# Decode attention plus MLP on one core: in each step a slice's scores are issued ahead of its values, and the values one slice later

## The chip, the cores and the metric

The kernel runs on one core of a Trainium2 chip. The core has a matrix engine (PE, TensorE), a vector engine (DVE, VectorE), an activation engine (ACT, ScalarE), GpSimd (POOL), and SyncE (SP), which here issues nearly all DMA transfers. Each engine works off its own list of instructions in order, and waits on semaphores where another engine or a transfer must be done first. PEld in a profile is PE's loading of weights (the stationary operand). The metric is the device time of one execution in microseconds (us).

## The reference, cut to what matters

One decode step (one token, batch 4) of two parallel blocks on the same normalised input:

```python
x = A_x                                   # (4, 1, 576) bf16
xn = layernorm(x)
# A: attention over the last W = 2048 positions of the cache, 32 query heads on 16 key/value heads of 128
q = (xn @ wq) as (4, 32, 1, 128)
scores = q . k_cache[:, :, -2048:, :] * 128 ** -0.5
o = softmax(scores) . v_cache[:, :, -2048:, :]
A = o as (4, 1, 4096) @ wo                # wo: 4096 x 576
# B: with one token the shifted groups of the mixer are zero, so hs = 0 and x1 = xn
B = xn + gelu(layernorm(xn) @ w3) @ w4    # w3: 576 x 4608, w4: 4608 x 576
out = x + A + B
```

What must be read is some 87 MB: 16 heads of keys and of values, 2 MB each, wq and wo of 4.7 MB each, w3 and w4 of 5.3 MB each. w1 and w2 aren't read.

## The kernel before

**Loads.** `load_kv` (L103) loads the keys of one key/value head for all four batches as one 128 x 8192 bf16 tile (2048 KB), the values likewise. Keys and values share a pool of six such buffers. The order is K0 K1 K2 V0 K3 V1 K4 V2 and so on to K15 V13 V14 V15; a quarter of wo goes ahead of every fourth V, w3 after V2, and w4 at the very end in six pieces (L141; the first has 18 of 36 blocks of rows, the last two have one each). All stand in SP's list, in that order. A load waits until the buffer that it takes over is free: K(t+3) takes that of K(t), free when DVE has turned its last slice; V(h+3) takes that of V(h), free when PE has used its last slice. `flush_loads` issues them at the end of each step.

**Steps.** One loop over t = 0 to 15 runs four heads at different stages, with hm = t-1, hv = t-2, hf = t-3, hp = t-4, and each step has four slices s = 0 to 3:

- `k_transpose` (L225): DVE turns a quarter of K(t), one slice ahead of its use, into one of three buffers kt;
- `k_mask` (L329) and `k_scores` (L338): PE adds the scores of slice s of head t into the PSUM tile S, four matmuls of 512 columns a slice. Two S tiles exist;
- softmax of head hm, spread over the slices: `sm_max` (L344, L346, DVE) at s = 0, `sm_maxT` (L351, PE) and `sm_neg` (L356, DVE) at s = 1, `sm_sub` (L360, PE) and `sm_exp` (L366, ACT) at s = 2, `sm_turn` (L372, DVE: the probabilities PT) and `sm_den` (L376, PE) at s = 3, `sm_rec` (L381, DVE) in the next step;
- `pv` (L390): PE multiplies slice s of PT(hv) with slice s of V(hv) into O, four matmuls that lie side by side in the array. The first one of a step waits for V(hv);
- head hf: `o_scale` (L397, ACT), `o_turn` (L403, PE), `o_sum` (L413, DVE); every fourth head `o_spread` (L422, PE), `o_pick` (L432, L435, DVE) and, a step later, `o_proj` (L183, PE: the product with a quarter of wo, into acc).

In step 7 the first product of the MLP (`mlp_g`, L456) with its turn and activation is put between. The schedule is manual: every engine's list has the instructions in the order in which the loop issues them.

**After the loop** the heads that are left are finished: the softmax of head 15, the values of heads 14 and 15, `o_turn`, `o_sum` and `o_spread` (L422, the tile R). Then `mlp_out` (L183) multiplies by w4 piece by piece, with `o_proj` of the last heads behind the first piece. These are pairs of 288-column matmuls with 8 rows of output, one of each pair into acc and one into acc_odd, which lie side by side in the array. ACT copies acc_odd (L606), DVE adds it to acc (L613), and SP stores 4.5 KB.

Of the kernel before, what the change touches and what calls it, by code (L numbers as in the profile page):

```python
# [22 lines left out]
def kernel(  # L23
# [32 lines left out]
    NSL = 4  # L56
# [165 lines left out]
    def k_transpose(h, s):  # L222
        src = kv_tiles["K", h][:].bitcast(I32)[:, s * SC:(s + 1) * SC, :].rearrange("p c (ib i) -> p ib c i", i=QD)
        kt = ktp.tile([P, 2, SC, QD], I32, tag="kt")
        nc.vector.transpose(out=kt[:], in_=src)  # L225
        kts[h, s] = kt
# [100 lines left out]
    def k_mask(h):  # L327
        S_ps[h] = ps_s.tile([P, NW], F32, tag="S", name="S")
        nc.tensor.matmul(out=S_ps[h][:].rearrange("p (c k) -> p c k", k=QD), lhsT=ohT[:],  # L329
                         rhs=negbig[:].unsqueeze(1).to_broadcast([B, SC, QD]),  # L330
                         start=True, stop=False, skip_group_check=True)

    def k_scores(h, s):
        kt = kts.pop((h, s))[:].bitcast(BF16)
        for ie in range(4):
            ib, e = divmod(ie, 2)
            z0 = (h * 4 + ie) * P + ZP - s * NJ
            nc.tensor.matmul(out=S_ps[h][:], lhsT=qz[:, z0:z0 + P],  # L338
                             rhs=kt[:, ib, :, e:2 * QD:2].rearrange("p c k -> p (c k)"),
                             start=False, stop=False, skip_group_check=True)  # L340

    def sm_max(h):
        mx = small.tile([P, 1], F32, tag="mx")
        nc.vector.reduce_max(out=mx[:], in_=S_ps[h][:], axis=AX.X)  # L344
        dm = small.tile([P, NG], BF16, tag="dm")
        nc.vector.tensor_scalar(out=dm[:], in0=sel_g[:], scalar1=mx[:, 0:1], scalar2=None, op0=ALU.mult)  # L346
        st["dm", h] = dm

    def sm_maxT(h):
        mg = ps_m.tile([NJ, NG], F32, tag="m", name="mg")  # L350
        nc.tensor.matmul(out=mg[:], lhsT=sel_jb[:], rhs=st.pop(("dm", h))[:], start=True, stop=True)  # L351
        st["mg", h] = mg

    def sm_neg(h):
        nm = small.tile([NJ, 1], BF16, tag="nm")
        nc.vector.reduce_max(out=nm[:], in_=st.pop(("mg", h))[:], axis=AX.X, negate=True)  # L356
        st["nm", h] = nm

    def sm_sub(h):
        nc.tensor.matmul(out=S_ps[h][:], lhsT=j_row[:], rhs=st.pop(("nm", h))[:, 0:1].to_broadcast([NJ, NW]),  # L360
                         start=False, stop=False, skip_group_check=True)

    def sm_exp(h):
        E[h] = ptp.tile([P, SC, QD], BF16, tag="e", name="E")
        rs = small.tile([P, 1], F32, tag="rs", bufs=3)
        nc.scalar.activation(out=E[h][:].rearrange("p c k -> p (c k)"), in_=S_ps.pop(h)[:], func=ACT.Exp, scale=scale,  # L366
                             accum_out=rs[:])
        st["rs", h] = rs

    def sm_turn(h):  # L370
        PT[h] = ptp.tile([P, SC, QD], BF16, tag="pt", name="PT")
        nc.vector.transpose(out=PT[h][:], in_=E.pop(h)[:])  # L372

    def sm_den(h):
        dn = ps_m.tile([P, 1], F32, tag="m", name="dn")
        nc.tensor.matmul(out=dn[:], lhsT=same_j[:], rhs=st.pop(("rs", h))[:], start=True, stop=True)  # L376
        st["dn", h] = dn

    def sm_rec(h):
        rd = small.tile([P, 1], F32, tag="rd", bufs=4)  # L380
        nc.vector.reciprocal(out=rd[:], in_=st.pop(("dn", h))[:])  # L381
        st["rd", h] = rd

    def pv(h, s):
        if s == 0:
            O_ps[h] = ps_o.tile([P, NSL, Dh], F32, tag="O", name="O")
        vn = kv_tiles["V", h][:].rearrange("p (s c) d -> p s c d", s=NSL)
        for g in range(NQD):
            c = s * NQD + g
            nc.tensor.matmul(out=O_ps[h][g * QD:(g + 1) * QD], lhsT=PT[h][:, c, :], rhs=vn[:, :, c, :],  # L390
                             start=(s == 0), stop=False, skip_group_check=True)
        if s == NSL - 1:
            PT.pop(h)

    def o_scale(h):
        O_sb[h] = bigp.tile([P, NSL, Dh], F32, tag="big", name="O_sb")
        nc.scalar.activation(out=O_sb[h][:], in_=O_ps.pop(h)[:], func=ACT.Copy, scale=st.pop(("rd", h))[:, 0:1])  # L397

    def o_turn(h):
        oT = ps_m.tile([P, NSL, P], F32, tag="m", name="oT")  # L400
        o = O_sb.pop(h)
        for s in range(NSL):
            nc.tensor.transpose(out=oT[:, s, :], in_=o[:, s, :], identity=ident_w[:, s * NJ:s * NJ + P])  # L403
        st["oT", h] = oT

    def o_sum(h):
        oT = st.pop(("oT", h))
        v = oT[:].rearrange("p s (g x) -> p (s g) x", g=NQD)[:, :, 0:NJ].rearrange("p g (b r) -> p b r g", r=rep)
        k = h % WOQ
        if k == 0:  # L410
            st["on"] = small.tile([P, WOH, B], BF16, tag="on", name="on")
        with nc.allow_low_precision("summed in float32"):
            nc.vector.reduce_sum(out=st["on"][:, k * rep:(k + 1) * rep, :].rearrange("p r b -> p b r"),  # L413
                                 in_=v, axis=AX.X)

    def o_spread(h):
        if h % WOQ < WOQ - 1:
            return
        on = st.pop("on")
        R = ps_m.tile([P, WOR, WOH, B], F32, tag="m", name="R")  # L420
        for i in range(WOR):
            nc.tensor.matmul(out=R[:, i].rearrange("p h b -> p (h b)"),  # L422
                             lhsT=sel_wo[:, i].rearrange("p h d -> p (h d)"),
                             rhs=on[:].rearrange("p h b -> p (h b)"), start=True, stop=True)
        st["R"] = R

    def o_pick(h):
        if h % WOQ < WOQ - 1:
            return
        R = st.pop("R")  # L430
        mk = small.tile([P, WOR, WOH, B], BF16, tag="mk")
        nc.vector.tensor_tensor(out=mk[:], in0=R[:],  # L432
                                in1=own[:].unsqueeze(1).unsqueeze(3).to_broadcast([P, WOR, WOH, B]), op=ALU.mult)
        with nc.allow_low_precision("one term is not zero"):
            nc.vector.reduce_sum(out=op[:, :, ROWS], in_=mk[:].rearrange("p i h b -> p i b h"), axis=AX.X)  # L435

    def o_proj(h):
        if h % WOQ < WOQ - 1:
            return
        for i in range(0, WOR, 2):  # L440
            acc_matmuls([(op[:, i + u, :], wo_tiles[h // WOQ][:, i + u, :]) for u in range(2)])
# [74 lines left out]
    for t in range(Hkv):  # L516
        hm, hv, hf, hp = t - 1, t - 2, t - 3, t - 4
        for s in range(NSL):
            if s == NSL - 1 and hm >= 0:
                sm_turn(hm)  # L520
            n = t * NSL + s + 1
            if n < Hkv * NSL:
                k_transpose(*divmod(n, NSL))

            if s == 0:
                if hm >= 0:
                    sm_max(hm)
                if hv >= 0:
                    sm_rec(hv)
                if hp >= 0:  # L530
                    o_pick(hp)
                if hf >= 0:
                    o_scale(hf)
                k_mask(t)
            elif s == 1 and hm >= 0:
                sm_maxT(hm)
            elif s == 2:
                if hm >= 0:
                    sm_sub(hm)
                    sm_exp(hm)  # L540
                if hf >= 0:
                    o_sum(hf)
            elif s == 3 and hm >= 0:
                sm_den(hm)
            if hv >= 0:
                pv(hv, s)
            k_scores(t, s)
            if s == 1:
                if hm >= 0:
                    sm_neg(hm)  # L550
                if hf >= 0:
                    o_turn(hf)
                if hp >= 0:
                    o_proj(hp)
            elif s == 3 and hf >= 0:
                o_spread(hf)
            if t == G_AT:
                if s < 3:
                    mlp_g(s)
                if s > 0:  # L560
                    mlp_turn(s - 1)
                if s == NSL - 1:
                    mlp_act()
        pos["free"] += 1
        if hv >= 0:
            pos["free"] += 1
        flush_loads()
# [77 lines left out]
```

## Time and profile before

| | us |
|---|---|
| median of six runs | 211.99 |
| the six runs | 211.51, 211.71, 211.73, 212.25, 212.36, 212.54 |
| profiled execution: its own time | 211.73 |
| profiled execution: span from first to last instruction | 210.0 |
| busy in the span: PE / PEld / DVE / ACT / POOL | 149.2 / 63.1 / 120.3 / 33.9 / 2.8 |
| moved by DMA | 87.32 MB, 416 GB/s over the span |
| idle time of PE ahead of values (L390) that a V transfer ended | 39.0, 12 times |
| mean granted clock of PE | 0.878 |

The page cuts the span into 40 slices of 5.25 us and gives the busy share of each engine, the clock that PE was granted, and the busy share of the DMA engines in tenths, 9 being 90% or more. The chain of waits follows the last instruction back to what released it, step by step. A row of the timeline is: start, duration, engine, line, operation, output <- inputs, shapes, number of instructions and, in brackets, how long the engine had been idle and what ended that. A row of the answer by stretches is: the stretch, its length, busy us (and number of instructions) of PE, PEld, DVE, ACT and POOL, the granted clock of PE as a share of the full one, the share of the DMA engines and GB/s.

### The profile page before, as it was taken

The numbers are of one execution on the slowest core, as the hardware profiler recorded it, in microseconds if no ns is written. First come the engines' busy times: TensorE is split into PE (matmuls) and PEld (weight loads), VectorE is DVE, ScalarE is ACT, GpSimd is POOL, SyncE is SP. The second block draws the span as 40 slices with busy tenths as digits, with TensorE's granted clock in tenths as the row PEclk, the third lists the DMA queues.
The fourth block names the chain that finished last, engine by engine and source line by source line (L and its number), as shares of the span: only waits on it lengthen the run. The fifth ranks groups of instructions, "written<-read, shape, count | busy, mean of one in ns | idle before, by whom it ended". The sixth has DMA issues, their size and how long they took to land.

```text
span 210.0 us, 2403 instructions
## 1 busy us (share of the span) xinstructions
PE 149.2 (71%) x955; PEld 63.1 (30%) x955; DVE 120.3 (57%) x217; ACT 33.9 (16%) x64; POOL 2.8 (1%) x15
## 2 busy tenths in 40 slices
PE   0277497839891009759999599697983956988884
PEld 0133132313340002214364144243431321443462
DVE  4831889782760082734806899849578391683310
ACT  7602201110220000201202122020211010202300
POOL 4010000000000000000000000000000000000000
PEclk9999679995998555967999999889999795999999
DMA  7999999999999999999999999999999999999992
GB/s 301 400 425 425 440 406 425 429 425 440 430 449 407 431 440 414 438 431 440 425 425 440 428 418 435 440 428 423 434 429 428 422 443 431 425 431 451 408 405 77
DMA packets 6659, 87.32 MB, mean 416 GB/s; under 512 B 748, under 2 KB 1016, under 8 KB 1656
## 3 DMA queue, kind: packets, MB, share of 16 engines
q1 hardware_dynamic: 6640, 87.17, 97.5%
q8 instruction: 7, 0.11, 0.2%
q14 instruction: 4, 0.03, 0.0%
q10 hardware_dynamic: 8, 0.00, 0.0%
HBM read 87.17 MB, written 0.00 MB: 415 GB/s over the span
## 4 chain that ended last, share of the span: by engine, by line
DMA 74%; PE 17%; DVE 6%; ACT 1%; issue 1%; SPq 0%; DVEq 0%
DMA vn<-in_A_v_cache_dram 37%; DMA w_sb<-in_B_w_dram 31%; PE S L338 6%; DMA wq_sb<-in_A_wq_dram 6%; DVE kt L225 3%; PE acc L183 2%; PE g_ps L456 2%; PE q_ps L285 2%; PE O L390 2%; DVE qz L317 1%; PE gT_ps L468 1%; PE oT L403 1%; DVE mx L344 1%; PE S L360 0%; PE qT_ps L300 0%
## 5 line engine op out<-in xcount | busy, mean ns | idle before, releaser
L225 DVE STREAM_TRANSPOSE kt<-kn 128x1024 int32<-128x1024 int32 x64 | 76.5, 1217 | 13.2 <-DMA kn<-in_A_k_cache_dram 12.1
L338 PE MATMUL S<-kt,qz 128*128 128x512 bf16 x256 | 78.6, 436 | 3.1 <-DVE kt L225 3.1
L390 PE MATMUL O<-vn,PT 128*32 128x512 bf16 x256 | 27.2, 425 | 39.1 <-DMA vn<-in_A_v_cache_dram 39.0
L338 PEld LDWEIGHTS <-qz 128*128 128x128 bf16 x256 | 21.7, 104 | 41.3 <-issue 25.3
L366 ACT ACTIVATE E<-S 128x512 bf16<-128x512 f32 x16 | 9.5, 597 | 121.8 <-PE S L360 121.8
L390 PEld LDWEIGHTS <-PT 128*32 128x32 bf16 x256 | 7.3, 94 | 47.3 <-issue 25.0
L372 DVE STREAM_TRANSPOSE PT<-E 128x512 bf16<-128x512 bf16 x16 | 11.4, 711 | 14.0 <-ACT E L366 14.0
L397 ACT ACTIVATE O_sb<-O,rd 128x512 f32<-128x512 f32 x16 | 11.0, 686 | 15.5 <-issue 11.0
L356 DVE TENSOR_REDUCE nm<-mg 8x1 bf16<-8x16 f32 x16 | 2.3, 146 | 18.6 <-PE mg L351 18.6
L413 DVE TENSOR_REDUCE on<-oT 128x8 bf16<-128x128 f32 x16 | 4.5, 280 | 12.1 <-PE oT L403 12.1
L403 PE MATMUL oT<-ident_w,O_sb 128*128 128x128 f32 x64 | 11.1, 302 | 0.3 <-ACT O_sb L397 0.3
L344 DVE TENSOR_REDUCE mx<-S 128x1 f32<-128x512 f32 x16 | 10.5, 657 | 1.3 <-PE S L338 1.3
L403 PEld LDWEIGHTS oT<-ident_w,O_sb 128*128 128x128 f32 x64 | 8.9, 158 | 5.2 <-issue 2.9
L183 PE MATMUL acc<-wo_sb,op 128*8 128x288 bf16 x56 | 7.5, 286 | 0.0
L376 PEld LDWEIGHTS dn<-rs,same_j 128*128 128x128 f32 x32 | 5.8, 188 | 2.9 <-ACT E L366 0.7
L360 PE MATMUL S<-nm,j_row 8*128 8x512 bf16 x16 | 6.3, 396 | 0.0
L183 PE MATMUL acc<-w_sb,gT 128*8 128x288 bf16 x38 | 5.3, 285 | 1.4 <-DMA w_sb<-in_B_w_dram 1.3
L329 PE MATMUL S<-negbig,ohT 4*128 4x512 bf16 x16 | 6.2, 385 | 0.0
L183 PEld LDWEIGHTS <-op 128*8 128x8 bf16 x64 | 4.7, 87 | 2.2 <-issue 0.5
L351 PE MATMUL mg<-dm,sel_jb 128*8 128x16 bf16 x16 | 2.8, 174 | 3.5 <-DVE dm L346 3.5
L285 PE MATMUL q_ps<-wq_sb,xnT 128*32 128x512 bf16 x40 | 4.5, 631 | 0.9 <-DMA wq_sb<-in_A_wq_dram 0.9
L474 DVE COPY g_x<-gT_ps 128x64 f32<-128x64 f32 (+1 forms) x3 | 0.6, 195 | 7.7 <-PE gT_ps L468 7.7
(93 smaller groups left out, 82.2 us busy)
## 6 DMA issues: line engine op xcount, KB each, us to landing
kn<-in_A_k_cache_dram SPq DMA_DIRECT2D x16, 2048.0 KB, 22.1
vn<-in_A_v_cache_dram SPq DMA_DIRECT2D x16, 2048.0 KB, 24.6
wo_sb<-in_A_wo_dram SPq DMA_DIRECT2D x4, 1152.0 KB, 25.5
w_sb<-in_B_w_dram SPq DMA_DIRECT2D x1, 4608.0 KB, 33.8
wq_sb<-in_A_wq_dram SPq DMA_DIRECT2D x1, 4096.0 KB, 12.6
w_sb<-in_B_w_dram SPq DMA_DIRECT2D x1, 2592.0 KB, 30.7
w_sb<-in_B_w_dram SPq DMA_DIRECT2D x2, 864.0 KB, 32.9
w_sb<-in_B_w_dram SPq DMA_DIRECT2D x2, 576.0 KB, 32.8
```

The lines of the kernel that those rows point to most:

```text
L183: nc.tensor.matmul(out=to[q:q + OR, :], lhsT=lhsT[:, NI - 1 - i:NI - 1 - i + OR], rhs=rhs[:, i * CW:(i + 1) * CW], start=start, stop=False ...
L225: nc.vector.transpose(out=kt[:], in_=src)
L285: nc.tensor.matmul(out=q_ps[r][g * QD:(g + 1) * QD, :], lhsT=xnT[:, k, :], rhs=wq_sb[:, col:col + NW], start=(j == 0), stop=False, skip_gr ...
L329: nc.tensor.matmul(out=S_ps[h][:].rearrange("p (c k) -> p c k", k=QD), lhsT=ohT[:], rhs=negbig[:].unsqueeze(1).to_broadcast([B, SC, QD]), ...
L338: nc.tensor.matmul(out=S_ps[h][:], lhsT=qz[:, z0:z0 + P], rhs=kt[:, ib, :, e:2 * QD:2].rearrange("p c k -> p (c k)"), start=False, stop=Fa ...
L344: nc.vector.reduce_max(out=mx[:], in_=S_ps[h][:], axis=AX.X)
L360: nc.tensor.matmul(out=S_ps[h][:], lhsT=j_row[:], rhs=st.pop(("nm", h))[:, 0:1].to_broadcast([NJ, NW]), start=False, stop=False, skip_grou ...
L366: nc.scalar.activation(out=E[h][:].rearrange("p c k -> p (c k)"), in_=S_ps.pop(h)[:], func=ACT.Exp, scale=scale, accum_out=rs[:])
L372: nc.vector.transpose(out=PT[h][:], in_=E.pop(h)[:])
L390: nc.tensor.matmul(out=O_ps[h][g * QD:(g + 1) * QD], lhsT=PT[h][:, c, :], rhs=vn[:, :, c, :], start=(s == 0), stop=False, skip_group_check ...
L397: nc.scalar.activation(out=O_sb[h][:], in_=O_ps.pop(h)[:], func=ACT.Copy, scale=st.pop(("rd", h))[:, 0:1])
L403: nc.tensor.transpose(out=oT[:, s, :], in_=o[:, s, :], identity=ident_w[:, s * NJ:s * NJ + P])
```

## The change

In each step the four score matmuls of slice s are issued ahead of the value matmuls, and the value matmuls of slice s move to slice s+1. Slice 0 has none; slice 3 has those of slices 2 and 3.

```diff
             elif s == 3 and hm >= 0:
                 sm_den(hm)
-            if hv >= 0:
-                pv(hv, s)
             k_scores(t, s)
+            if hv >= 0 and s > 0:
+                pv(hv, s - 1)
+                if s == NSL - 1:
+                    pv(hv, s)
             if s == 1:
                 if hm >= 0:
                     sm_neg(hm)
```

PE's list of a step from t = 4 on (a step without a product with wo or w3) was: mask, values 0, scores 0, maxT, values 1, scores 1, o_turn, sm_sub, values 2, scores 2, sm_den, values 3, scores 3. It becomes: mask, scores 0, maxT, scores 1, values 0, o_turn, sm_sub, scores 2, values 1, sm_den, scores 3, values 2, values 3. The lists of the other engines have the same instructions in the same order. The code after the loop is unchanged; it stands two lines further down.

## The prediction

> **What bounds the kernel now.** I read the page's slices first, then the chain of waits, the landing times of the K tiles, the tail of the timeline, and last the clock in stretches of 3.41 us.
>
> ```profile
> PEclk9999679995998555967999999889999795999999
> DMA  7999999999999999999999999999999999999992
> DMA 74%; PE 17%; DVE 6%; ACT 1%; issue 1%; SPq 0%; DVEq 0%
> ```
>
> The 16 DMA engines are full from the second slice to the last but one. TensorE's clock falls to half in the middle, and nothing in the DMA row answers to that. The chain in order of time (start, length, what) shows the pace, and the answer on the K tiles, in the second fence, the margin:
>
> ```profile
> 150.55 24.48 DMA vn<-in_A_v_cache_dram
> 175.03 0.02 issue
> 175.04 31.12 DMA w_sb<-in_B_w_dram
> 206.16 0.04 issue
> ```
>
> ```profile
> DMA to landing us min/median/max: 14.3/22.1/36.0
> ```
>
> V12 (head 12's values) landed at 175.03; V13 let PE go at 184.76 (below). Two 2048 KB loads lie between: 4.86 us each. So a K tile waits at least 14.3 - 4.86 = 9.4 us in the queue: 9.4 us is how much later a buffer may come free before the stream breaks. From the same pace V14 lands at 189.6, V15 at 194.5, w4's first piece (2592 KB, 6.15 us) at 200.6; its row says 200.67. The tail of PE's timeline:
>
> ```profile
> 184.76 0.40 PE L390 MATMUL O<-vn,PT 128*32 128x512 bf16 x4 [0.99 <-DMA vn<-in_A_v_cache_dram]
> ...
> 192.04 1.07 PE L338 MATMUL S<-kt,qz 128*128 128x512 bf16 x4
> 193.04 0.40 PE L390 MATMUL O<-vn,PT 128*32 128x512 bf16 x4
> ...
> 196.55 1.05 PE L390 MATMUL O<-vn,PT 128*32 128x512 bf16 x16
> ...
> 199.48 0.35 PE L422 MATMUL R<-on,sel_wo 128*128 128x32 bf16 x8 [0.38 <-DVE on L413]
> 200.67 0.28 PE L183 MATMUL acc<-w_sb,gT 128*8 128x288 bf16 x1 [0.85 <-DMA w_sb<-in_B_w_dram]
> ...
> 206.69 0.66 PE L183 MATMUL acc<-w_sb,gT 128*8 128x288 bf16 x4
> 206.90 0.40 ACT L606 ACTIVATE odd<-acc_odd 8x288 f32<-8x288 f32 x1 [8.51 <-PE acc_odd L183]
> ```
>
> The end needs both the last pieces of w4 and PE's 42 pairs of L183 matmuls. The pairs start 0.118 us apart, 42 x 0.118 = 4.96 us, so PE could have passed the last pair at 205.63; it did at 206.69. **PE's slack in the tail is 1.06 us**, and everything after that pair (ACT, DVE, the store) follows it. The clock, asked in stretches of 3.41 us between its steps:
>
> ```profile
> 117.87:121.28 3.41, 1.61 (x13) 0.91 (x13) 3.38 (x7) 0.00 (x0) 0.00 (x0) 1.00 0.98 418
> 131.52:134.94 3.42, 1.57 (x13) 0.47 (x13) 2.90 (x5) 0.00 (x0) 0.00 (x0) 1.00 0.97 417
> 134.94:138.35 3.41, 3.41 (x15) 1.48 (x14) 1.42 (x3) 0.00 (x0) 0.00 (x0) 0.50 1.02 437
> 162.24:165.66 3.42, 2.92 (x13) 0.68 (x13) 0.33 (x2) 0.00 (x0) 0.00 (x0) 0.50 0.97 415
> 165.66:169.07 3.41, 3.41 (x27) 1.78 (x23) 2.02 (x4) 0.69 (x2) 0.00 (x0) 1.00 1.01 429
> 90.56:93.98 3.42, 2.39 (x12) 0.58 (x13) 0.00 (x0) 0.00 (x0) 0.00 (x0) 0.50 0.98 422
> 93.98:97.39 3.41, 3.41 (x15) 1.49 (x14) 1.41 (x3) 0.00 (x0) 0.00 (x0) 0.50 1.01 432
> 203.20:206.62 3.42, 2.88 (x46) 1.95 (x43) 0.00 (x0) 0.00 (x0) 0.00 (x0) 1.00 0.74 290
> ```
>
> Column two is PE's busy time, the last but two the granted clock. 1.61 us busy kept the full clock; 1.57 us lost it for the next stretch; 2.92 us busy brought it back, 2.39 us didn't.
>
> **The change, part by part.** No instruction is added or removed: 14 steps (t = 2 to 15) reorder 16 value and 16 score matmuls each on PE. SP, DVE, ACT and POOL keep their lists; no load passes another.
>
> Scores ahead. mask, scores 0, maxT and scores 1 of step t no longer stand behind the wait for V(t-2). They need K(t), which lands 4.86 us before it, and slices that DVE turns at 1.22 us each. About 1.01 + 1.01 us of scores leaves the time after V. By the slices alone that is a gain of 2 us per step; in the stream it is worth 0, because the DMA row is full and the loads come at 4.86 us whatever PE does.
>
> Values later. The wait for V now stands ahead of o_turn, o_proj, sm_sub and scores 2 and 3, as before; only scores 0 and 1 escaped it. sm_sub still follows V, so E and PT come some 2 us earlier after V, not later. V(t-2)'s buffer is freed by the step's last matmul: after V lands, the step has 2 us less to do, so V(t+1) is issued up to 2 us earlier. K(t)'s last turn needs scores 0 done (three kt buffers), which no longer waits for V: K(t+3) is issued earlier too, or at the same time where the turn is queued behind DVE's own waits. Bounds for both: 2 us earlier to 0.66 us later (two value slices at 0.33 now end the step), against 9.4 us of margin. Cost 0 in the stream. The granted clock in mid-kernel may be lost more often or less; a step at half clock is one of 162.75 to 170.2 us, also inside the margin.
>
> The tail, where PE does count. Step 15: from V13 at 184.76 to the step's end at 193.04 are 8.28 us. The two score slices gone, 6.2 us: the end at 191.0, the last score at 190.3 (two value slices follow it). From the last score to PT(15) the chain max, dm, mg, nm, sub, exp, turn took 196.55 - 193.04 = 3.5 us: PT(15) at 193.8. V15 lands at 194.5, so the last values start at 194.5 instead of 196.55, and R ends at 197.8 instead of 199.83. **w4's piece still lands at 200.67: PE's wait of 0.85 us becomes 2.9 us.** Nothing is gained, and PE is idle just ahead of the only stretch where its speed sets the end.
>
> What the idle costs. Call e the end of a 3.41 us stretch; where e lies against the program I take as equally likely anywhere. PE's busy rows from 194.5 are 1.64, 0.66 and 0.35 us, then nothing to 200.67. A stretch holds 1.57 us or less if e lies between 199.0 and 202.25: 95% of the 3.41 us. Then the clock is half until the next stretch of at least some 2.65 us busy (between 2.39 and 2.92) ends. At half clock the weight loads of the first scores start at 24.55, 24.98 and 25.41, 0.43 us apart for 512 columns; 288 columns are then 0.24 us a pair (estimate from those rows) against 0.118. Each us of half clock after 200.67 loses 0.508 us; from the sum goes the slack of 1.06:
> - e from 199.0 to 199.9 (26%): two stretches, half clock until about 206.2, 5.6 us: 2.84 - 1.06 = +1.8;
> - e from 199.9 to 200.67 (23%): 2.6 to 3.4 us: +0.3 to +0.67, mean +0.48;
> - e from 200.67 to 202.25 (46%): 3.41 us: +0.67;
> - else 0.
> Mean 0.47 + 0.11 + 0.31 = **+0.89 us**.
>
> The Trainium skill (TensorE: Matmul & The Clock Gate, "HAM oscillation") says that idle gaps over about 3.4 us are what loses the clock. By it a gap of 2.9 us costs nothing and the time would stay. The trace speaks against that: after 131.52 the longest wait was 1.85 us and the clock went.
>
> **The base.** The profiled execution took 211.73 us (span 210.0, 1.73 around it), 0.26 under the median 211.99. The six runs lie in two groups, 211.51 to 211.73 and 212.25 to 212.54, 0.73 apart in the mean, near the price of one half-clock stretch. I suspect the old tail is caught in part of the runs already; no trace here shows it. Scaling 0.89 by 0.73/0.67 gives 0.97: 211.73 + 0.97 = **212.7 us**, +0.33%.
>
> **Rivals.**
> 1. The idle in the tail costs nothing (the other side: not slower). It decides at 2.09 us of half clock after 200.67 (1.06/0.508): less is covered by the slack. For it: the old tail's stretches were kept; against it: the count above. Time 211.5 to 212.3, as before.
> 2. The 8-column matmuls of L183 don't bring the clock back. 42 x 0.24 = 10.1 us instead of 4.96: +4.06, 215.8. Against it: they kept the clock in the stretch 203.20 to 206.62.
> 3. Buffers come free late and the stream breaks: beyond 9.4 us each us of delay is a us; a delay of 10.5 us would give 212.8. Nothing in the reorder delays a release by more than 0.66 us.
> 4. The stream itself gets faster by earlier issues: it has no gap after 1.2 us to fill; if anything, under 0.7 us from 211.73, 211.1.
>
> **How the numbers follow.** About 0.3% (0.64 us) is what a measurement of this kernel tells from no change. Tail caught, 62%: of these the median lies beyond +0.64 us over 211.99 in 45 and short of it in 17, since one stretch alone is worth only +0.67 on 211.73. Rival 1: 24% (22 same, 2 faster by the scatter). Rival 2: 7%. Rival 3: 3%. Rival 4: 4%. Slower 0.55, same 0.39, faster 0.06. Range: low end rival 1's 211.5, high end two stretches in most runs, 211.73 + 2.0 = 213.7; rivals 2 and 4 and their like are the 2 in 10 left out.
>
> **What would show it.** The DMA row still full, w4's first L183 still at about 200.7. The last values near 194.5 instead of 196.55; PE waiting 2 to 3 us for w4's first piece; a clock of 0.5 in the stretch after it with pairs 0.24 us apart, and ACT's copy of acc_odd starting after 207.5 instead of 206.90. Wrong if the clock stays at 1.00 from 199 to 207, if the last values don't move, or if the DMA row has a dip in mid-kernel.

## The result, and the profile after

| | before | changed |
|---|---|---|
| median, us | 211.63 (48 runs, 211.43 to 212.57) | 212.49 (24 runs, 211.86 to 213.69) |
| profiled execution, its own time | 211.73 | 212.63 |
| its span | 210.0 | 210.9 |

The ratio is 1.0047, 95% interval 1.0037 to 1.0057: the changed kernel is slower by 0.86 us in the median. The single runs stand in groups. Before: 39 runs at 211.43 to 211.83, nine at 212.07 to 212.57. Changed: one at 211.86, fourteen at 212.18 to 212.56, nine at 213.0 to 213.69.

The page of the changed kernel, its slices:

```profile
PEclk9999589976996559979999699999997695899769
DMA  8999999999999999999999999999999999999990
```

The DMA row is as full as before, to the last slice but one. The answer on the K tiles:

```profile
DMA to landing us min/median/max: 17.2/23.9/38.8
```

The shortest time from issue to landing has grown from 14.3 to 17.2 us: the loads are issued earlier, queue longer, and nothing is won by it. The first piece of w4 lands at 200.72 (200.63 before), the last at 207.04 (206.90). The loss is behind that. The tail of the timeline:

```profile
191.89 0.40 PE L390 MATMUL O<-vn,PT 128*32 128x512 bf16 x4
...
194.75 1.90 PE L390 MATMUL O<-vn,PT 128*32 128x512 bf16 x16 [0.63 <-DMA vn<-in_A_v_cache_dram]
196.59 1.88 PE L403 MATMUL oT<-ident_w,O_sb 128*128 128x128 f32 x8
198.84 0.35 PE L422 MATMUL R<-on,sel_wo 128*128 128x32 bf16 x8 [0.38 <-DVE on L413]
200.76 0.28 PE L183 MATMUL acc<-w_sb,gT 128*8 128x288 bf16 x1 [1.57 <-DMA w_sb<-in_B_w_dram]
...
202.60 0.44 PE L183 MATMUL acc<-w_sb,gT 128*8 128x288 bf16 x1
202.61 0.45 PE L183 MATMUL acc_odd<-w_sb,gT 128*8 128x288 bf16 x1
202.84 0.44 PE L183 MATMUL acc<-w_sb,gT 128*8 128x288 bf16 x1
...
207.58 0.65 PE L183 MATMUL acc<-w_sb,gT 128*8 128x288 bf16 x4
207.79 0.40 ACT L608 ACTIVATE odd<-acc_odd 8x288 f32<-8x288 f32 x1 [10.35 <-PE acc_odd L183]
```

The last values (x16) start at 194.75 instead of 196.55, and PE then waits 1.57 us for w4 instead of 0.85. From 201.6 the pairs are 0.24 us apart (202.60, 202.84) instead of 0.12, and the four single matmuls at the end come at 207.58 instead of 206.69. All the pieces of w4 had landed 0.5 us earlier: PE is now last. The stretches of 3.41 us between the steps of the clock (columns as before: length, busy us of five engines, granted clock, DMA share, GB/s):

```profile
191.35:194.77 3.42, 2.48 (x32) 1.08 (x25) 1.70 (x7) 2.06 (x4) 0.00 (x0) 1.00 1.02 439
194.77:198.18 3.41, 3.41 (x23) 1.90 (x24) 0.29 (x1) 0.69 (x1) 0.00 (x0) 0.50 1.03 444
198.18:201.59 3.41, 1.46 (x25) 1.09 (x25) 1.14 (x3) 0.00 (x0) 0.00 (x0) 1.00 0.92 382
201.59:205.01 3.42, 3.42 (x33) 2.05 (x30) 0.00 (x0) 0.00 (x0) 0.00 (x0) 0.50 0.99 406
205.01:208.42 3.41, 3.22 (x48) 2.25 (x44) 0.20 (x2) 0.40 (x1) 0.00 (x0) 1.00 0.23 86
```

The clock is lost twice. The stretch 194.77 to 198.18 costs only waiting time (the values take 1.90 instead of 1.05 us, R (L422) starts 4.09 us behind them instead of 2.93, and the wait for w4 shrinks by about as much). The stretch 201.59 to 205.01 lies in the L183 pairs and costs the time.

### The profile page after: what moved, and what is told of

It is laid out like the page before. It is cut to its first block, busy times and chain, and to the rows that moved or that the text cites. A ratio compares the mean times of both kernels' runs of the same rounds, so it can differ in the third digit from the quotient of the medians.

```text
span 210.9 us, 2397 instructions
## 1 busy us (share of the span) xinstructions
PE 154.9 (73%) x955; PEld 61.4 (29%) x955; DVE 120.3 (57%) x217; ACT 33.9 (16%) x64; POOL 2.8 (1%) x15
## 4 chain that ended last, share of the span: by engine, by line
DMA 71%; PE 21%; SPq 2%; DVE 2%; issue 1%; ACT 0%; DVEq 0%
DMA kn<-in_A_k_cache_dram 29%; DMA vn<-in_A_v_cache_dram 28%; DMA w_sb<-in_B_w_dram 15%; PE S L338 7%; PE acc L183 4%; PE O L390 3%; PE g_ps L456 2%; PE oT L403 2%; SPq L103 2%; DVE kt L225 1%; PE S L360 1%; PE gT_ps L468 1%; DVE mx L344 1%; PE dn L376 1%; SPq L125 0%
## 5 line engine op out<-in xcount | busy, mean ns | idle before, releaser
L338 PE MATMUL S<-kt,qz 128*128 128x512 bf16 x256 | 77.3, 430 | 23.1 <-DVE kt L225 23.1
L338 PEld LDWEIGHTS <-qz 128*128 128x128 bf16 x256 | 23.3, 108 | 56.2 <-issue 39.6
L390 PE MATMUL O<-vn,PT 128*32 128x512 bf16 x256 | 24.4, 425 | 8.6 <-DMA vn<-in_A_v_cache_dram 8.6
L390 PEld LDWEIGHTS <-PT 128*32 128x32 bf16 x256 | 6.1, 96 | 30.6 <-issue 29.8
L403 PE MATMUL oT<-ident_w,O_sb 128*128 128x128 f32 x64 | 13.0, 340 | 0.0
L183 PE MATMUL acc<-wo_sb,op 128*8 128x288 bf16 x56 | 7.9, 294 | 0.0
L183 PE MATMUL acc<-w_sb,gT 128*8 128x288 bf16 x38 | 6.3, 333 | 1.6 <-DMA w_sb<-in_B_w_dram 1.6
L376 PEld LDWEIGHTS dn<-rs,same_j 128*128 128x128 f32 x32 | 5.0, 197 | 4.3 <-issue 3.6
L376 PE MATMUL dn<-rs,same_j 128*128 128x1 f32 x32 | 6.2, 262 | 0.0
L183 PE MATMUL acc_odd<-w_sb,gT 128*8 128x288 bf16 x34 | 5.9, 340 | 0.0
L183 PEld LDWEIGHTS <-op 128*8 128x8 bf16 x64 | 4.9, 93 | 2.5 <-issue 0.5
L351 PEld LDWEIGHTS <-sel_jb 128*8 128x8 bf16 x16 | 1.3, 83 | 14.4 <-DVE dm L346 12.3
```

The costliest lines, as they stand in the source:

```text
L183: nc.tensor.matmul(out=to[q:q + OR, :], lhsT=lhsT[:, NI - 1 - i:NI - 1 - i + OR], rhs=rhs[:, i * CW:(i + 1) * CW], start=start, stop=False ...
L338: nc.tensor.matmul(out=S_ps[h][:], lhsT=qz[:, z0:z0 + P], rhs=kt[:, ib, :, e:2 * QD:2].rearrange("p c k -> p (c k)"), start=False, stop=Fa ...
```

## The experiments

Theory: the new order makes PE reach w4 early, the idle time costs it the clock, and the half clock behind w4's first piece is the loss. Main rival: the order itself costs, by what it puts later in each step. Each timed kernel was compared with the kernel before on the same chip.

### Fill the idle time of the new order

```diff
+    def keep_busy(n):
+        idle = ps_s.tile([P, NW], F32, tag="S", name="idle_fill")
+        for _ in range(n):
+            nc.tensor.matmul(out=idle[:], lhsT=qz[:, 0:P], rhs=sel_wo[:, 0:4].rearrange("p i h d -> p (i h d)"),
+                             start=True, stop=True)
...
     o_spread(hl)
     o_pick(hl)
+    keep_busy(8)
     mlp_out(*pieces[0])
```

> The new order with eight throwaway matmuls of 512 columns (2.0 us at full clock) on PE between o_spread of head 15 and the first piece of w4. Nothing else changes. Clock theory: PE is no longer idle ahead of w4, keeps its full clock from w4's first piece on, and the time goes back to that of the kernel before: 211.5 to 211.8 us, ratio 0.998 to 1.001, with no runs beyond 212.7. Rival, that the new order itself costs the time (buffers, later values, the softmax chain): the extra matmuls can only add, 212.5 us or more, ratio 1.004 or more.

Measured: 211.59 us (211.48 to 211.75, 11 runs), ratio 0.9994 (0.9986 to 1.0003). The whole loss is gone with eight matmuls more. Its stretches:

```profile
197.21:200.62 3.41, 2.52 (x20) 1.22 (x19) 1.14 (x3) 0.00 (x0) 0.00 (x0) 1.00 0.92 384
200.62:204.04 3.42, 3.35 (x56) 2.59 (x57) 0.00 (x0) 0.00 (x0) 0.00 (x0) 1.00 1.01 420
```

The stretch ahead of w4 has 2.52 us of busy PE, and the one behind keeps 1.00. The order of the steps is the changed one throughout, so the order as such costs nothing that shows.

### The same in the old order

`keep_busy(4)` at the same place in the kernel before.

> The old order with four such matmuls (1.0 us) at the same place, where PE waited 0.85 us for w4. Clock theory: the runs of the kernel before at 212.07 to 212.57 (10 of 48) are those whose tail lost the clock; they vanish, and all runs lie at 211.4 to 211.85, median 211.5 to 211.65, ratio 0.999 to 1.000. Rival, that the scatter of the kernel before has another cause (DMA): about a fifth of the runs stays above 212.0.

Measured: 211.59 us (211.40 to 212.22, 11 runs), ratio 1.0003 (0.9994 to 1.0011). One run of eleven is above 212.0; on this chip the kernel before had two of 35. (The expectation says 10 of 48 runs at 212.07 to 212.57; they are nine.) This settles nothing about the late runs of the old order: neither that they vanish nor that they stay.

### Where in the loop the order matters

Two kernels, shown against the kernel before:

```diff
+            ahead = t < Hkv - 1        # second kernel: t == Hkv - 1
-            if hv >= 0:
+            if hv >= 0 and not ahead:
                 pv(hv, s)
             k_scores(t, s)
+            if hv >= 0 and ahead and s > 0:
+                pv(hv, s - 1)
+                if s == NSL - 1:
+                    pv(hv, s)
```

> The new order in steps 2 to 14, the old one in step 15. Clock theory: the tail meets V15 and w4 nearly as in the kernel before (last values near 196.5 us, PE waiting about 0.9 us for w4), so 211.6 to 211.9 us, ratio 1.000 to 1.002; a little more if PE, idle for some 2 us ahead of V13, loses the clock in step 15. Rival, a cost of the order in each of its 14 steps: 13/14 of the loss stays, ratio 1.004.

> The old order in steps 2 to 14, the new one in step 15 alone. Clock theory: step 15 ends about 1 us earlier than in the kernel before, the last values start near 195 us, PE waits 2 to 2.6 us for w4 and the clock is lost in most runs: 212.2 to 212.5 us, ratio 1.003 to 1.005. Rival, a cost of the order in each of its 14 steps: 1/14 of the loss, ratio 1.000 to 1.001.

Measured: steps 2 to 14 alone 211.68 us, ratio 1.0010 (1.0001 to 1.0020); step 15 alone 212.05 us, ratio 1.0020 (1.0010 to 1.0031), with six of twelve runs at 212.26 to 212.59. Thirteen steps of the new order cost a fifth of the loss, and the last step alone costs two fifths, so a price per step is out. In the profiled execution of steps 2 to 14 (211.56) the clock was lost all the same, from 196.48 to 199.90: the last values started at 196.44 and took 1.90 us instead of 1.05, and the expected wait of 0.9 us for w4 was gone. By 199.90 the clock was full again, and the pairs ran at full pace. Half clock ahead of w4 cost nothing. Step 15 alone falls short of the 1.003 expected. Its timeline shows where it differs:

```profile
185.74 0.17 PE L351 MATMUL mg<-dm,sel_jb 128*8 128x16 bf16 x1 [0.44 <-DVE rd L381]
...
196.21 1.05 PE L390 MATMUL O<-vn,PT 128*32 128x512 bf16 x16
...
199.14 0.35 PE L422 MATMUL R<-on,sel_wo 128*128 128x32 bf16 x8 [0.38 <-DVE on L413]
200.86 0.40 PE L183 MATMUL acc<-w_sb,gT 128*8 128x288 bf16 x1 [1.37 <-DMA w_sb<-in_B_w_dram]
```

The old step 14 ends too late for step 15's first scores to be done before V13 (landed at 184.95; values 0 of step 15 start at 186.84); the last values start at 196.21, hardly earlier than in the kernel before, and the wait is 1.37 us, not 2 to 2.6. By this the full effect needs step 14 and step 15 in the new order; no kernel with just these two was run.

### The filler at another place

```diff
+            if t == Hkv - 2 and s == 1:
+                keep_busy(14)          # 288 columns each, into the bank of acc_odd
             if hv >= 0 and s > 0:
```

> The new order with fourteen throwaway matmuls of 288 columns (1.7 us at full clock) where PE waits 3.2 us for V12 in step 14, none in the tail. Clock theory: they keep the clock in step 14 at most; the wait for w4 in the tail is as long as in the changed kernel, so 212.3 to 212.7 us, ratio 1.003 to 1.006. Rival, that extra matmuls help by keeping PE going anywhere, or by step 14's slow pace: back to 211.6, ratio 1.000.

Measured: 212.44 us (211.61 to 213.29, 10 runs), ratio 1.0036 (1.0020 to 1.0053). The filler kept the clock in step 14 (0.50 from 174.29 to 181.11 in the changed kernel, 1.00 here), and the loss stayed. Here the extra matmuls helped only ahead of the end, where PE's pace sets the time. The tail shows it with the wait at its full length:

```profile
197.93:201.35 3.42, 0.76 (x14) 0.59 (x15) 0.75 (x2) 0.00 (x0) 0.00 (x0) 1.00 0.89 371
201.35:204.76 3.41, 3.41 (x34) 2.10 (x30) 0.00 (x0) 0.00 (x0) 0.00 (x0) 0.50 1.00 412
```

### Less work in the old order

```diff
         kt = kts.pop((h, s))[:].bitcast(BF16)
+        if h == Hkv - 1 and s < 2:
+            return
         for ie in range(4):
```

> The old order with work left out: the score matmuls of slices 0 and 1 of head 15 (8 matmuls, 2.0 us at full clock) are not done, so head 15's part of the output is another one. Step 15 ends 2 us earlier, as in the new order, and PE waits longer for w4. Clock theory: less work makes it slower: 212.2 to 212.5 us, ratio 1.003 to 1.005, with the clock at half behind w4's first piece. Rival, that the new order costs by what it puts later: without it no loss, 211.5 to 211.65 us, ratio 0.999 to 1.000.

Measured: 212.38 us (211.42 to 213.56, 12 runs), ratio 1.0044 (1.0027 to 1.0062): eight matmuls fewer, no value moved, and the same loss with the same two groups (six runs at 212.12 to 212.41, five at 213.11 to 213.56). So a loss of this size needs nothing that the new order puts later. That it comes from PE being early is argued from the times alone. The profiled execution was the one run without the loss (211.42): it had lost the clock earlier, from 185.56 to 188.98, its last values started at 195.98, its wait for w4 was 1.10 us, and the clock stayed full in the tail. Neither the long wait nor the half clock is shown for this kernel.

### Useful work in the idle time

```diff
+    o_proj(hl)
     mlp_out(*pieces[0])
-    o_proj(hl)
```

> The new order with o_proj of head 15 (8 pairs, 0.95 us) ahead of w4's first piece instead of behind it: useful work goes into the wait, and PE's slack in the tail grows from 1.06 to 2.0 us. Clock theory: one half-clock stretch (1.73 us lost) is now covered, 211.5 to 211.8 us in those runs; only runs with more than 3.9 us at half clock stay late, up to 212.6. Median ratio 0.999 to 1.001. Rival, that the loss has nothing to do with PE's pace in the tail: 212.5 us, ratio 1.004.

Measured: 211.65 us (211.48 to 211.73, 11 runs), ratio 0.9995 (0.9986 to 1.0004). All runs lie together, those that the expectation allowed up to 212.6 included. Swapping two lines takes the loss away without extra work:

```profile
197.50 0.35 PE L422 MATMUL R<-on,sel_wo 128*128 128x32 bf16 x8 [0.38 <-DVE on L413]
198.82 0.29 PE L183 MATMUL acc<-wo_sb,op 128*8 128x288 bf16 x1 [0.97 <-DVE op L435]
...
200.85 0.28 PE L183 MATMUL acc<-w_sb,gT 128*8 128x288 bf16 x1 [0.88 <-DMA w_sb<-in_B_w_dram]
...
206.90 0.40 ACT L608 ACTIVATE odd<-acc_odd 8x288 f32<-8x288 f32 x1 [10.49 <-PE acc_odd L183]
```

Two waits of 0.97 and 0.88 us stand in place of one of 2.8, this execution kept the clock, and ACT starts at 206.90 as in the kernel before. Whether the other runs kept the clock or paid for it out of the larger slack can't be told from their times.

### Both

Four filler matmuls and `o_proj(hl)` ahead of w4's first piece, in the new order.

> The new order with four throwaway matmuls (1.0 us) behind o_spread and then o_proj of head 15 ahead of w4's first piece. Clock theory: the clock is kept, slack is 2.0 us, and the DMA stream alone sets the end: all runs at 211.4 to 211.75, median 211.5 to 211.6, ratio 0.998 to 1.000; no run like those of the kernel before at 212.0 to 212.6. Rival: 212.5 us or more.

Measured: 211.70 us (211.38 to 211.94, 11 runs), ratio 1.0001 (0.9993 to 1.0010). The expected median of 211.5 to 211.6 was missed, and four runs are above 211.75. It isn't better than either alone. No version beats the kernel before: the last piece of w4 lands at 206.93 here (206.90 before), and that is the floor of the versions near 211.6.

### What the two groups of runs are

> The changed kernel once more, one look with its profile. Clock theory: the last L183 pair comes 0.508 us later for each us of half clock after w4's first piece, less the slack of 1.06: with one stretch of 3.41 us the time is about 212.3 to 212.6 us; with two stretches in the tail (5 us or more at half clock) 213.0 to 213.7 us. Rival, that the runs at 213.0 to 213.7 have another cause: such a run shows one stretch or none, or a late w4.

> As the look before this one: the same kernel, the position of the 3.41 us stretches against the program left to chance. One stretch at half clock in the tail: 212.3 to 212.6 us; two: 213.0 to 213.7 us; under 2.09 us at half clock: 211.4 to 211.8 us.

> As the two looks before this one: one stretch at half clock in the tail 212.3 to 212.6 us; two 213.0 to 213.7 us; under 2.09 us at half clock 211.4 to 211.8 us.

> The changed kernel once more, for a look at a run of the group at 213.0 to 213.7 us (9 of the first 24). Clock theory: if the time falls into that group, the tail shows two adjacent stretches at half clock, 5 us or more behind w4's first piece; if it is 212.2 to 212.6, one stretch, and the group stays without a profile. Rival, another cause of the group: such a time with one stretch.

Measured, with the time from w4's first L183 to ACT's copy of acc_odd, and how long PE had half clock in it:

| execution | time, us | wait for w4 | half clock behind w4's first piece | first L183 to ACT |
|---|---|---|---|---|
| before | 211.73 | 0.85 | 0 | 6.22 |
| changed | 212.63 | 1.57 | 3.41 | 7.02 |
| again 1 | 212.47 | 2.83 | 3.41 | 7.02 |
| again 2 | 212.30 | 2.20 | 3.41 | 7.02 |
| again 3 | 212.62 | 2.22 | 3.41 | 7.01 |
| again 4 | 213.16 | 2.79 | 5.18 | 7.87 |

The fourth of these (again 4) met the late group, and its stretches are these:

```profile
195.36:198.77 3.41, 1.63 (x20) 1.20 (x17) 1.43 (x4) 0.69 (x1) 0.00 (x0) 1.00 0.96 410
198.77:202.18 3.41, 1.77 (x16) 1.04 (x17) 0.00 (x0) 0.00 (x0) 0.00 (x0) 0.50 0.97 405
202.18:205.59 3.41, 3.41 (x32) 1.89 (x29) 0.00 (x0) 0.00 (x0) 0.00 (x0) 0.50 0.87 352
205.59:209.00 3.41, 3.14 (x48) 2.07 (x42) 0.28 (x2) 0.40 (x1) 0.00 (x0) 1.00 0.10 35
```

Here a stretch ended at 198.77, ahead of w4: the next one was half idle and didn't bring the clock back, the one after it did. One stretch costs 0.80 us, two (5.18 us of them behind w4's first piece) 1.65 us. Where the stretches lie differs from run to run of the same program: the half clock began at 201.59, 201.88, 200.62, 200.75 and 198.77. In these five executions that is what separates the times; of the late group there is this one profile.

## Why the prediction was right, point by point

- **The stream, cost 0: right.** The DMA row is full, w4 lands within 0.15 us of before, and K's shortest time from issue to landing grew from 14.3 to 17.2 us. Rivals 3 (a late buffer) and 4 (a faster stream) are out.
- **The tail earlier by 2 us: right.** The last values at 194.5 predicted; 194.75 in the changed kernel's profile and 194.35 to 195.23 in the four more profiles. In two of these PT(15) and not V15 decided, against the forecast: the values started at 194.93 and 195.23 without a wait for V15.
- **PE's wait for w4 at 2.9 us: nearly.** 2.20, 2.22, 2.79 and 2.83 in four profiles, 1.57 in the other. There the clock was lost earlier too, behind the stretch that ends in the wait for V15, and the slower values ate part of the wait. That earlier loss wasn't foreseen.
- **The clock lost, 95%: right.** All five profiles of the changed kernel show half clock behind w4's first piece, and 23 of its 24 timed runs lie above 212.1. The kernel with the filler shows that the loss hangs on the idle time, the times of the one with less work say that a loss of this size needs no new order. Rival 1 (the idle costs nothing) fell. So did rival 2: the clock comes back during L183 pairs alone (201.59 to 205.01 all L183, then 1.00).
- **The measure for losing it, 1.57 us busy in a stretch: wrong as a measure.** The stretch 191.35 to 194.77 had 2.48 us busy and lost the clock; 197.87 to 201.29 of the kernel with `o_proj` first had 1.58 us and kept it. The busy column counts more than the streaming: a row of four value matmuls is 0.40 us, where 512 columns at 0.42 ns are 0.21. Counted by streamed columns (0.83 ns each at half clock, from 0.24 us for 288, and half of that at full), side-by-side matmuls once, the fourteen profiled executions have 553 full-clock stretches after 20 us: of 91 with less than 36.5% streaming, 90 lost the clock (12 of them run past the last instruction); of 428 with more than 41.5% none did; 34 lie between, and 18 of those lost it. The two bounds were read from these same stretches, and the one exception lies in a tail: 195.05 to 198.46 of again 1, with 25%. By this count the old tail's stretches of 0.39 and 0.41 lay where it can go either way. The old number still gave the right forecast, in part by luck: ahead of the half clock behind w4's first piece the five profiles have stretches of 0.81 to 1.63 us busy, 7 to 38% streaming, on both sides of 1.57 us and of the lower bound.
- **The price of one stretch, +0.67: measured +0.80.** The failed term is the pace of the pairs: 42 x 0.118. From 200.67 to 202.75 the old profile has 17 steps, 0.122 each, so the work is 5.14 us and the slack 0.88 instead of 1.06. 3.41 us at half clock lose 1.67, less 0.88 is 0.79 (measured 0.80); 5.18 us lose 2.54, less 0.88 is 1.66 (measured 1.65).
- **The phases: one sized too small.** Two stretches were put at 26% of the runs; 9 of 24 (38%) are in that group. The profile of that group has its stretch ending at 198.77, ahead of the 199.0 where the forecast let the band begin.
- **The base: the number that failed most.** Six runs, three of them late, gave 211.99; 48 give 211.63. The forecast of 212.7 is 0.21 us off, but the change against the base is 0.86 us, where the text had +0.71 on 211.99. That 212.7 came so near is partly luck: it is a mean over the phases, on a base 0.15 us above the median of the 39 runs that aren't late, 211.58, with a price per stretch that was too small and two stretches too rare. That the old tail is caught in part of its runs (nine of 48 are late) stays a suspicion: no profile of a late run of the old kernel exists, and the filler in the old order didn't decide it. The nearest row is that of steps 2 to 14: with the old step 15 its stretch of 193.07 to 196.48 (36.5% streaming) lost the clock.
- **The skill's rule.** The Trainium skill (TensorE: Matmul & The Clock Gate, "HAM oscillation") has idle gaps over about 3.4 us losing the clock; by it the loss would be 0. Here it was lost with waits of 1.57 to 2.83 us in five of five profiles. What the same page says of the window in "Part 1" (3413 ns, free-running) agrees: stretches of 3.41 us that lie elsewhere in each execution.

## What to carry to other kernels

When a kernel waits for its stream of loads, ask what PE does between its last wait and the end: work that comes earlier only lengthens the wait, and a wait of some 2 us just ahead of the final matmuls can halve their pace. Put work that is due anyway into that wait (here a swap of two lines), and only if there is none, throwaway matmuls. Read groups in the single runs as a sign of something whose position is left to chance, and take enough runs for the base before a change of 0.5% is judged.

## What the runs showed of the hardware that wasn't expected

- Taking eight matmuls out made the old kernel slower by 0.44% (0.27 to 0.62%), and putting eight into the new one made it faster than the change by 0.9 us.
- The clock was lost with PE busy 2.48 of 3.41 us by the profile's count, where the busy time was made of side-by-side value matmuls, transposes and short matmuls.
- The clock came back only after a stretch that was mostly work: the stretch from 198.77 to 202.18, with 1.77 us busy, didn't bring it back, the next one, full, did. With a stretch ending 1.64 us ahead of the work (198.77 against 200.41), PE ran 5.18 us at half clock; ending behind its start, 3.41 us.
